# A transformer block with attention and eight experts on one core: sums of x from DRAM, a fourth pair buffer, one stay of tails, the fifth tile amid the chain

## The chip, the core and the metric

The kernel runs on one core of one Trainium2 chip. The core has five engines, each with its own instruction queue: TensorE (PE, matrix products into the eight PSUM banks), VectorE (DVE), ScalarE (ACT), GpSimd (POOL) and SyncE (SP, which here issues nearly all DMA). They meet through semaphores. The metric is the device time of one execution in microseconds (us), lower is better. The kernel before was timed three times: 2646.43 us in the median, 2645.69 to 2650.43 us.

## The reference

```python
xn = layernorm(x)                       # x: 1 x 2048 x 448, float32
# A: attention, 16 heads of 28
q, k, v = split(xn @ wqkv)              # wqkv: 448 x 1344
p = softmax(q @ k.T * 28 ** -0.5)       # 2048 x 2048 for each head
A = concat_heads(p @ v) @ wo            # wo: 448 x 448
# B: eight experts, all eight chosen (top 8 of 8)
gates = softmax(xn @ w_gate)            # 448 x 8
for e in range(8):
    B += gates[:, e] * (silu(xn @ w1[e]) @ w2[e])   # w1: 8 x 448 x 1792, w2: 8 x 1792 x 448
out = x + A + B
```

## The kernel before

**Numbers.** TensorE works in float16. To keep float32 quality each operand is split into a high and a low float16 part, and a product is the sum of three matmuls (high by high, high by low, low by high).

**Two streams.** After a first phase (norm of x, transposes, q, k, v, gates: about 110 us) two streams run side by side to the end. The *experts* go through 24 groups (`GROUPS`: three per expert, of 5, 5 and 4 tiles of 128 rows of w1) and in each group through 4 blocks of 512 tokens: 96 *units*. *Attention* goes through 256 tiles (one head, 128 queries), each in two halves of 1024 keys.

**A unit** (`unit`) computes four of the group's tiles for 512 tokens with a scheme of the Strassen kind on part of the inner dimension: seven products instead of eight, on sums of quarters of w1 (buffers `wa`) and sums of quarters of x (`T1` to `T4`, kept for all tokens in the tile `xt`). In the code's words: A11 into bank b1; ACT copies b1 to bank b2 (L1146); S1 into b3; ACT copies b3 to `s5` (L1148); S2 onto b1; DVE puts b1 + s5 into b3 (L1151); A12 onto b2; S3 onto b1; DVE puts b1 + s5 into b4 (L1155); S4 onto b3; A22 onto b1. This is called the *chain* here: each step on b1 has to wait until the copy or the sum before it has read b1. The products are L1105. The rest of the inner dimension goes on top as plain products (`plain`, L1121) and as *tails* (`tails`, L1132): the last 64 rows, which need only half of the PE's 128 rows, so that two such matmuls run in the two halves of the array at once. There are two stays of tails in a unit: b2 and b3 after S4, b1 and b4 at the end.

**After it** every bank goes through `silu`: ACT's tanh from the bank into a float32 tile `t` (L1202), DVE's (tanh + 1) times z (L1205, which frees the bank), ACT's high part `hh` (L1208), POOL's low part `hl` (L1209). A group of five has one more tile (`single`, L1177: 11 matmuls of 512 columns), which runs ahead of its unit. When a unit's parts stand, `summed` multiplies them by w2 for four token tiles (L1265, three matmuls of 448 columns for each tile of the group) and DVE adds the result, weighted by the gate, to `acc` (L1276).

**Weights.** While a group is computed, the next one's w1 and w2 are loaded, their largest magnitudes taken by DVE (L405) and brought to all partitions over DRAM (`mxs`, `scmg`), and then scaled and split by ACT and POOL (`split_w1`, `split_w2`). There are three `wa` buffers for pairs of tiles (`RWA`), two pairs in a group.

**Attention.** `score` writes 128 x 1024 scores into the two banks of kind "s" (L1363, two matmuls); DVE multiplies them by minus the scale in place and takes the minimum (L1367, a custom instruction with an accumulator that is then read out); ACT takes the exponential (L1383) and the high part (L1391); DVE the low part (L1386); SP transposes both by DMA (L1404); `weigh` multiplies by V (L1438 on four column strips of 32, L1445), `project` by wo (L1531).

**Order.** All instructions are jobs in a planner (`Plan`): a job has an engine, a cost in ns, a priority `v` (the units' and the attention's priorities are spread over the run), dependencies and buffers. At the kernel's build it plays the jobs through with these costs, gives each engine that falls free the ready job of lowest priority whose buffers fit, and writes the instructions in that order. On the chip every engine then works through its list as it stands. PSUM banks are given out by kind: "u" (b1, b3) any of 3, 2, 7, 6; "e" (b2, b4) 4 and 5; "z" and "y" 6, 7, 3, 2 (and more for "y").

## Time and profile before

| what | value |
|---|---|
| median of three runs | 2646.43 us (2645.69 to 2650.43) |
| the profiled execution's own time | 2647.7 us |
| its span, first to last instruction | 2645.9 us |
| granted TensorE clock | 0.999 |
| busy: PE, DVE, ACT, POOL | 2596.9, 2350.1, 2069.8, 1356.0 us |
| DMA: mean rate, share of the 16 engines in the main queue | 160 GB/s, 73.9% |

The rows that follow in the prediction come from that one execution. "L1105" is line 1105 of the kernel before. A row of groups reads: line, engine, operation, what it writes and reads, shape, count, busy time, mean ns of one, and the idle time of the engine ahead of it with what ended it. A row of the timeline reads: start, duration, engine, line, operation, shape, count, and in brackets an idle time. Matmuls follow each other before the one ahead has ended: the distance of two starts is what one costs, the duration is longer.

### The profile page before, as it was taken

Reading aid. Unit: us, or ns where it says so; the run is one execution under the profiler, and the core shown is the slowest. Engines: PE = TensorE matmul, PEld = TensorE weight load, DVE = VectorE, ACT = ScalarE, POOL = GpSimd, SP = SyncE. Lnnn points to the kernel's source line nnn. Section 1 sums busy time; section 2 is a strip of 40 time slices with the busy share of each in tenths; the row PEclk is TensorE's granted clock in tenths of the full one; section 3 lists DMA queues with packets and bytes.
Section 4 is the critical chain, followed back from the end, with each engine's and each line's share of the span. In section 5 each row is a group of like instructions: output and inputs, shape, how many; then the busy total and the mean of one; then the engine's idle time right before and its main releaser. Section 6 shows DMA issues by size and latency. Waiting matters only on the chain.

```text
span 2645.9 us, 54809 instructions
## 1 busy us (share of the span) xinstructions
PE 2596.9 (98%) x20863; PEld 1597.2 (60%) x20863; DVE 2350.1 (89%) x3567; ACT 2069.8 (78%) x2993; POOL 1356.0 (51%) x1377
## 2 busy tenths in 40 slices
PE   9999999999999999999999999999999999999999
PEld 4565665566656666556666656655566666656656
DVE  8779899998998899989999899998899998998873
ACT  5578778777887877888888877878778888787772
POOL 2345535544655444555454655555546555466462
PEclk9999999999999999999999999999999999999999
DMA  9657677687777778678887787877787677877741
GB/s 258 176 117 169 151 169 169 146 168 160 157 176 157 161 160 166 160 161 157 170 172 155 157 166 170 171 152 168 145 175 174 159 178 159 174 173 146 151 104 60
DMA packets 1237303, 424.46 MB, mean 160 GB/s; under 512 B 1156144, under 2 KB 1201712, under 8 KB 1237040
## 3 DMA queue, kind: packets, MB, share of 16 engines
q1 hardware_dynamic: 1236480, 420.94, 73.9%
q8 instruction: 164, 2.69, 0.5%
q14 instruction: 99, 0.81, 0.1%
q10 hardware_dynamic: 560, 0.02, 0.0%
HBM read 119.72 MB, written 15.23 MB: 51 GB/s over the span
## 4 chain that ended last, share of the span: by engine, by line
PE 54%; DVE 9%; ACT 3%; issue 2%; POOL 1%; DMA 1%; SPq 0%; DVEq 0%; POOLq 0%; ACTq 0%
PE banks L1265 22%; PE banks L1105 10%; PE banks L1121 8%; PE banks L1363 5%; PE banks L1177 3%; DVE banks L1367 3%; PE banks L1445 3%; DVE pl L1386 2%; PE banks L1438 2%; PE banks L1132 1%; DVE t L1205 1%; ACT pf L1383 1%; PE banks L1531 1%; DVE acc L1276 1%; ACT ph L1391 1%
## 5 line engine op out<-in xcount | busy, mean ns | idle before, releaser
L1209 POOL TENSOR_TENSOR hl<-t,hh 128x512 f16<-128x512 f32 x448 | 594.8, 1336 | 810.5 <-ACT hh L1208 753.6
L1265 PE MATMUL banks<-w,hh 128*128 128x448 f16 x3576 | 969.7, 353 | 2.2 <-DVE acc L1276 1.6
L1383 ACT ACTIVATE pf<-banks,mx 128x1024 f32<-128x1024 f32 x512 | 568.4, 1110 | 287.3 <-DVE mx L1367 248.7
L1386 DVE SCALAR_TENSOR_TENSOR pl<-pf,ph 128x1024 f16<-128x1024 f32 x512 | 719.4, 1407 | 39.7 <-ACT ph L1391 38.7
L1367 DVE CUSTOM_DVE_ANT_0 banks<-banks,zero,cneg 128x1024 f32<-128x1024 f32 x512 | 658.1, 1285 | 69.5 <-PE banks L1363 56.2
L1265 PE MATMUL banks<-w,hl 128*128 128x448 f16 x1788 | 630.2, 352 | 0.0
L1391 ACT ACTIVATE ph<-pf 128x1024 f16<-128x1024 f32 x512 | 539.0, 1053 | 4.9
L1265 PEld LDWEIGHTS <-hh 128*128 128x128 f16 x3576 | 339.9, 98 | 335.9 <-issue 27.4
L1105 PEld LDWEIGHTS <-wa 128*128 128x128 f16 x4032 | 391.9, 98 | 141.6 <-issue 42.4
L1121 PE MATMUL banks<-xs,wc 128*128 128x256 f16 x3072 | 399.0, 273 | 0.0
L1202 ACT ACTIVATE t<-banks,the 128x512 f32<-128x512 f32 x448 | 298.4, 681 | 101.3 <-POOL hl L1209 50.1
L1105 PE MATMUL banks<-xt,wa 128*128 128x256 f16 x2304 | 313.2, 273 | 26.7 <-ACT banks L1146 14.3
L1205 DVE SCALAR_TENSOR_TENSOR t<-t,banks 128x512 f32<-128x512 f32 x448 | 298.4, 680 | 46.1 <-ACT t L1202 45.1
L1121 PEld LDWEIGHTS <-wc 128*128 128x128 f16 x3072 | 294.3, 98 | 62.4 <-issue 15.8
L1363 PE MATMUL banks<-K,Q 112*128 112x512 f16 x1024 | 305.9, 380 | 11.2 <-ACT pf L1383 10.4
L1276 DVE SCALAR_TENSOR_TENSOR acc<-banks,gwe,acc 128x448 f32<-128x448 f32 x383 | 257.2, 677 | 59.0 <-PE banks L1265 58.1
L1208 ACT ACTIVATE hh<-t 128x512 f16<-128x512 f32 x448 | 273.9, 623 | 18.0 <-DVE t L1205 10.2
L1265 PEld LDWEIGHTS <-hl 128*128 128x128 f16 x1788 | 174.4, 98 | 164.2 <-POOL hl L1209 0.5
L1105 PE MATMUL banks<-xs,wa 128*128 128x256 f16 x1728 | 236.5, 273 | 0.0
L611 POOL TENSOR_TENSOR w<-r,w 128x448 f16<-128x448 f32 x112 | 136.5, 1228 | 76.2 <-ACT w L608 74.7
L1177 PE MATMUL banks<-xs,wc 128*128 128x512 f16 x704 | 164.9, 379 | 0.0
L1363 PEld LDWEIGHTS <-Q 112*128 112x128 f16 x1024 | 94.1, 98 | 83.7 <-issue 30.5
(173 smaller groups left out, 2603.7 us busy)
## 6 DMA issues: line engine op xcount, KB each, us to landing
K<-qk SPq DMA_DIRECT2D x512, 56.0 KB
r<-in_B_w_dram SPq DMA_DIRECT2D x16, 1120.0 KB
V<-vs SPq DMA_DIRECT2D x64, 256.0 KB
r<-in_B_w_dram SPq DMA_DIRECT2D x16, 960.0 KB
Q<-qk SPq DMA_DIRECT2D x256, 28.0 KB
r<-in_B_w_dram SPq DMA_DIRECT2D x8, 896.0 KB
r<-in_B_w_dram SPq DMA_DIRECT2D x8, 768.0 KB
r<-in_B_w_dram SPq DMA_DIRECT2D x32, 160.0 KB
```

The source lines that it names most:

```text
L1105: nc.tensor.matmul(bank()[:, q * HC : (q + 1) * HC], w, xx, start=(start and q == 0 and i == 0), stop=True, skip_group_check=True,)
L1121: nc.tensor.matmul(bank()[:, q * HC : (q + 1) * HC], ww, xx, start=False, stop=True, skip_group_check=True,)
L1202: add("ACT", 686, lambda: nc.scalar.activation(t(), z(), AF.Tanh, scale=th_()[:, 0:1]), v, r=[z, th_], w=[t])
L1205: lambda: nc.vector.scalar_tensor_tensor(t(), t(), 1.0, z(), op0=ALU.add, op1=ALU.mult),
L1209: add("POOL", 1159, lambda: nc.gpsimd.tensor_tensor(hl(), t(), hh(), ALU.subtract), v, r=[t, hh], w=[hl])
L1265: nc.tensor.matmul(y()[:, 0:D], a, wv, start=(i == 0 and u == 0), stop=(i == g - 1 and u == 2))
L1276: lambda: nc.vector.scalar_tensor_tensor(acc[:, n, :], y()[:, 0:D], gb()[:, n : n + 1], acc[:, n, :], op0=ALU.mult, op1=ALU.add),
L1363: nc.tensor.matmul(b()[:, cs], q()[:, q0 : q0 + P], k()[:, cs], start=True, stop=True)
L1367: nc.vector.tensor_tensor_reduce(b(), b(), zero.to_broadcast([P, 2 * C]), cneg, HUGE, op0=ALU.add, op1=ALU.min, accum_out=m()[:, n, j : j ...
L1383: nc.scalar.activation(p(), s(), AF.Exp, bias=m()[:, n, j : j + 1], scale=-1.0)
L1386: nc.vector.scalar_tensor_tensor(l()[:, js], p(), P_SCALE, h()[:, js], op0=ALU.mult, op1=ALU.subtract)
L1391: add("ACT", 1060, lambda: nc.scalar.activation(h()[:, js], p(), AF.Copy, scale=P_SCALE), v, r=[p], w=[(h, j)])
```

## The change

- **Sums of x.** `xt`, 16 KB in every partition, goes. The sums are worked out after the first phase (`sums_of_x`, now in `moe`), written to DRAM (`xd`), and each unit has its own 4 KB buffer out of two, loaded from `xd` (`sums_x`, 512 KB per load, 94 loads); the first two units get theirs directly.
- **Buffers.** `wa` 3 to 4, `w2` 6 to 7, `hh` and `hl` 7 to 8 (now rings in one tile `hr`), `t` 2 to 3.
- **Tails.** One stay at the end of a unit for all four banks, eight matmuls; all four `silu` follow it.
- **Fifth tile.** `single` stands between S1 and S2 of its unit.
- **Scores.** The scale is put into q and k when they are split. DVE takes the minimum of the raw scores by a `tensor_reduce` that writes nothing back.
- **Scales of weights.** w1 and w2 get theirs apart, w1's earlier; the splitting starts earlier; POOL's first part of a pair is three jobs. Some costs and constants of the planner differ.

```diff
-RWA, RWC, RW2, RH, RHC, RT, RPP, RPF = 3, 4, 6, 7, 2, 2, 2, 2
+RWA, RWC, RW2, RH, RHC, RT, RPP, RPF = 4, 4, 7, 8, 2, 3, 2, 2
...
-    mxs = dp.tile([len(GROUPS), P, 2], F32, name="mxs")
+    mxs = dp.tile([len(GROUPS), 2, P, 2], F32, name="mxs")
     vs = dp.tile([H, P, NC, TPC * 64], F16, name="vs")
+    xd = dp.tile([NC, P, 8, HC], F16, name="xd")
...
-    xt = mp.tile([P, 8 * XT], F16, name="xt")
+    hr = mp.tile([P, 2 * RH * C], F16, name="hr")
...
-                add("ACT", 600, lambda pq=pq, qh=qh: nc.scalar.activation(qh(), pq(), AF.Copy), v(), r=[pq], w=[qh])
+                def high(pq=pq, qh=qh, sc_=sc_):
+                    nc.scalar.activation(qh(), pq(), AF.Copy, scale=sc_)
+                def low(pq=pq, qh=qh, ql=ql, sc_=sc_):
+                    nc.vector.scalar_tensor_tensor(ql(), pq(), sc_, qh(), op0=ALU.mult, op1=ALU.subtract)
...
             v = go([b3], strassen(b3, S1, T1, True))
-            add("ACT", 610, lambda: nc.scalar.activation(s5(), b3(), AF.Copy), v, r=[b3], w=[s5])
+            add("ACT", 595, lambda: nc.scalar.activation(s5(), b3(), AF.Copy), v, r=[b3], w=[s5])
+            done = amid(last, v0) or done
             tick()
...
             go([b3], strassen(b3, S4, B22), plain(b3, 0, 1))
-            v = go([b2, b3], tails((b2, b3), 0))
-            silu(gi, b, (0, 0), b2, v)
-            silu(gi, b, (0, 1), b3, v)
             tick()
             go([b4], plain(b4, 1, 1))
             go([b1], strassen(b1, A22, T4), plain(b1, 1, 0))
-            v = go([b1, b4], tails((b1, b4), 1))
+            v = go([b2, b3, b1, b4], tails(((b2, 0, 0), (b3, 0, 1), (b1, 1, 0), (b4, 1, 1))))
+            silu(gi, b, (0, 0), b2, v)
+            silu(gi, b, (0, 1), b3, v)
             silu(gi, b, (1, 0), b1, v)
             silu(gi, b, (1, 1), b4, v)
...
+        def sums_x(gi, b, v):
+            XS_[gi, b] = x = buf("mp", [P, 8, HC], F16, f"xt{gi}_{b}", tag="xt", bufs=2)
+            if not gi and b < 2:
+                sums_of_x(b, x, v)
+                return
+            dma(lambda: x(), lambda: xd[b], v, r=[("xd", b, 0), ("xd", b, 1)], w=[(x, 0), (x, 1)], kb=512)
...
+                todo = [(SLOT_A, scale_w1, gi + 1)]
+                todo += [(SLOT_A + 2 + 2 * i, split_w1, gi + 1, i) for i in range(len(W1S[g1]))]
+                todo += [(SLOT_B, scale_w2, gi + 1)]
...
             for b in range(NC):
-                if g > 4:
-                    single(gi, b)
-                unit(gi, b, tick)
+                g1, b1 = (gi, b + 1) if b + 1 < NC else (gi + 1, 0)
+                if 0 < g1 < len(GROUPS) or b1 > 1:
+                    sums_x(g1, b1, at(spent[0]))
+                unit(gi, b, tick, lambda after, v: single(gi, b, after, v) if g > 4 else None)
...
-                nc.vector.tensor_tensor_reduce(
-                    b(), b(), zero.to_broadcast([P, 2 * C]), cneg, HUGE,
-                    op0=ALU.add, op1=ALU.min, accum_out=m()[:, n, j : j + 1],
-                )
-            add("DVE", 1292, top, v, r=["cexp"], w=[b, (m, n, j)], more=58)
+                nc.vector.tensor_reduce(m()[:, n, j : j + 1], b(), op=ALU.min, axis=AX.X)
+            add("DVE", 1215, top, v, r=[b], w=[(m, n, j)])
...
+V0 = 20.0
+AHEAD, SLOT_A, SLOT_B = 0.0, 1, 6
```

What this does to the order is shown at three places: the second unit of the run on PE, where the chain and the tails stand; a later unit's `silu` on ACT; and SP's queue. Lines of the kernel after the change have other numbers: there L1084 are the products of the chain, L1100 the plain ones, L1111 the tails, L1156 the fifth tile, L1408 the scores, L1446 the transposes of the exponentials.

On PE, the second unit before: the last product of A11 (it reads `xs`) and the first of S1 (S1 and S2, twelve products that read `xt`, follow each other with nothing between), and the first of its two stays of tails (`wc` are the plain weights of a pair of tiles).

```order
L1105 MATMUL banks<-xs,wa_2_978 128x256
L1105 LDWEIGHTS wa_0_954
L1105 MATMUL banks<-xt,wa_0_954 128x256
...
L1121 MATMUL banks<-xs,wc_2_1044 128x256
L1132 LDWEIGHTS wc_0_1005
L1132 MATMUL banks<-xs,wc_0_1005 128x256
...
L1132 MATMUL banks<-xs,wc_2_1044 128x256
L1121 LDWEIGHTS wc_0_1005
L1121 MATMUL banks<-xs,wc_0_1005 128x256
```

Between A11 and S2 there stand S1's six matmuls only. After the change the same unit, from the last product of S1 to the first of S2:

```order
L1084 MATMUL banks<-xt_1_861,wa_2_964 128x256
L1156 LDWEIGHTS wc_4_933
L1156 MATMUL banks<-xs,wc_4_933 128x512
...
L1408 MATMUL banks<-K_1_1500,Q_1468 128x512
L1156 LDWEIGHTS wc_4_933
...
L1156 MATMUL banks<-xs,wc_4_933 128x512
L1084 LDWEIGHTS wa_0_943
L1084 MATMUL banks<-xt_1_861,wa_0_943 128x256
```

The eleven matmuls of the fifth tile and a pair of scores now stand between S1 and S2; the unit's tails are one run of eight matmuls at its end.

On ACT, the second unit of the tenth group before, from the first tanh of its four banks to the last (`t_1_00` to `t_1_11`; `pf`, `ph` are exponentials, `hh` high parts):

```order
L1202 ACTIVATE t_1_00_14086<-banks,the_13587 128x512
L1391 ACTIVATE ph_14032<-pf_1_14068 128x1024
L1202 ACTIVATE t_1_01_14105<-banks,the_13587 128x512
...
L1208 ACTIVATE hh_1_00_14127<-t_1_00_14086 128x512
L1383 ACTIVATE pf_0_14130<-banks,mx_14108 128x1024
L1391 ACTIVATE ph_14140<-pf_0_14130 128x1024
L1202 ACTIVATE t_1_10_14148<-banks,the_13587 128x512
L1208 ACTIVATE hh_1_01_14175<-t_1_01_14105 128x512
L1383 ACTIVATE pf_1_14179<-banks,mx_14108 128x1024
L1208 ACTIVATE hh_1_10_14217<-t_1_10_14148 128x512
L1202 ACTIVATE t_1_11_14235<-banks,the_13587 128x512
```

and after (`r` and `wa` are the next group's weights, `hr` holds the high parts):

```order
L1240 ACTIVATE t_1_00_13928<-banks,the_12546 128x512
L1240 ACTIVATE t_1_01_13941<-banks,the_12546 128x512
L1240 ACTIVATE t_1_10_13943<-banks,the_12546 128x512
L553 ACTIVATE r_10_13371<-r_10_13371,scoa_13832 128x4x256
L580 ACTIVATE wa_2_13948<-r_10_13371 128x128
L580 ACTIVATE wa_2_13948<-r_10_13371 128x256
L1425 ACTIVATE pf_0_13972<-banks,mx_13501 128x1024
L1247 ACTIVATE hr<-t_1_00_13928 128x512
L1433 ACTIVATE ph_13985<-pf_0_13972 128x1024
L1247 ACTIVATE hr<-t_1_01_13941 128x512
L1240 ACTIVATE t_1_11_14008<-banks,the_12546 128x512
```

Three of the four tanh follow each other at once, the fourth comes seven instructions later; before they came one or two at a time.

On SP after the change, around one load of sums (`xt_0`, for the first unit of a group):

```order
L1446 DMA_TRANSPOSE tl_9745<-pl_9984 128x16x128
L1446 DMA_TRANSPOSE th_10194<-ph_10058 128x16x128
L382 DMA xt_0_10216<-xd 128x2048
L1446 DMA_TRANSPOSE tl_10294<-pl_10119 128x16x128
L1497 DMA_TRANSPOSE tt_10310<-lt_10297 128x4x128
L382 DMA V_10328<-vs 128x1024
```

Before, the transposes of two exponentials followed each other there, and no load of sums stood in the queue; now one stands ahead of a transpose in each unit.

## The prediction

> **What bounds the kernel now.** I read the page first, then PE's waits, then the timeline of one unit.

> ```profile
> span 2645.9 us, 54809 instructions
> PE 2596.9 (98%) x20863; PEld 1597.2 (60%) x20863; DVE 2350.1 (89%) x3567; ACT 2069.8 (78%) x2993; POOL 1356.0 (51%) x1377
> PE 54%; DVE 9%; ACT 3%; issue 2%; POOL 1%; DMA 1%; SPq 0%; DVEq 0%; POOLq 0%; ACTq 0%
> ```

> PE is busy for all but 49 us of the span, and it is 54% of the chain that ended last. DVE at 89% looks close to a bound, but the rows of its waits say that it waits for PE:

> ```profile
> DVE acc L1276 <- PE banks L1265: 58.1, 61, 2.2
> DVE banks L1367 <- PE banks L1363: 56.2, 72, 3.2
> ```

> So time is won only where PE stops or spends more than its columns need. Its own waits (us in total, times, longest), complete but for 3 us in small rows:

> ```profile
> PE banks L1105 <- ACT banks L1146: 14.3, 20, 1.9
> PE banks L1363 <- ACT pf L1383: 10.4, 11, 1.8
> PE banks L1105 <- DVE banks L1151: 9.9, 11, 1.8
> PE banks L1438 <- DVE u L1463: 2.8, 3, 1.9
> PE banks L1265 <- DVE acc L1276: 1.6, 2, 1.3
> PE banks L728 <- DVE one L722: 1.2, 1, 1.2
> PE banks L1105 <- DVE t L1205: 1.1, 1, 1.1
> ```

> Rows one and three, 24.2 us, are the chain: S2 waits until ACT has copied b1, S3 until DVE has read it. What a matmul costs, and what PE loses without a wait, stands in the timeline of a unit of the first group (start, duration, ...), its last row ACT's:

> ```profile
> 133.27 0.82 PE L1105 MATMUL banks<-xs,wa 128*128 128x256 f16 x6
> 133.92 0.82 PE L1105 MATMUL banks<-xt,wa 128*128 128x256 f16 x6
> 135.61 0.81 PE L1105 MATMUL banks<-xt,wa 128*128 128x256 f16 x6 [0.87 <-ACT banks L1146]
> 136.26 0.82 PE L1105 MATMUL banks<-xs,wa 128*128 128x256 f16 x6
> 141.93 1.04 PE L1121 MATMUL banks<-xs,wc 128*128 128x256 f16 x8
> 142.90 0.39 PE L1132 MATMUL banks<-xs,wc 64*128 64x256 f16 x4
> 143.23 0.55 PE L1265 MATMUL banks<-w,hh 128*128 128x448 f16 x2
> 134.98 0.58 ACT L1146 ACTIVATE banks<-banks 128x512 f32<-128x512 f32 x1
> ```

> Six matmuls of 256 columns take 0.65 (133.27 to 133.92), 0.109 each. S1 begins at 133.92 and S2 could follow at 134.57; it begins at 135.61. PE lost 1.04 there, where the bracket says 0.87: a stop costs some 0.16 more than its row, because the last matmul's modelled end covers that much. ACT began its copy at 134.98 and was through at 135.56: from the start of S1, 133.92, PE would have needed 1.7 us of other work. And the tails: eight plain matmuls from 141.93 are through at 142.80 (8 x 0.109), the tails begin at 142.90, 0.10 late; they need 2 x 0.109 = 0.22 (two at a time, in two halves of the array) and the next begins 0.33 later, 0.11 late. A stay costs 0.20 beside its work.

> **The change part by part.**

> *One stay of tails.* The matmuls are the same in number and width, and in the run of eight the halves still alternate, so pairs still run together. From 192 stays, 96 go: 96 x 0.20 = 19.2 us of PE time, on the engine that bounds. From below: if a stay of eight lost its pairing it would cost 4 x 0.109 more, which the unchanged order of halves excludes. I take -19.2.

> *Fifth tile amid the chain.* In the order before, 46 of the 96 units have less than 1.6 us of matmuls between the end of A11 and S2 (counted over the whole PE order, each matmul at its distance in the trace); after, 18 have. Between S2 and S3 24 units have less than that before, 9 after. S2's wait costs 14.3 + 20 x 0.16 = 17.5, S3's 9.9 + 11 x 0.16 = 11.7. Shrinking both in proportion saves 17.5 x 28/46 = 10.7 and 11.7 x 15/24 = 7.3: -18.0 us. The bounds are 0 (ACT and DVE are late for reasons of their own, whatever stands between) and -29.2 (all of it). I take the proportion: the wait quoted above stands where only S1 covers ACT's copy, and there the fifth tile's 11 matmuls and a score now stand.

> *The minimum of the scores.*

> ```profile
> L1367 DVE CUSTOM_DVE_ANT_0 banks<-banks,zero,cneg 128x1024 f32<-128x1024 f32 x512 | 658.1, 1285 | 69.5 <-PE banks L1363 56.2 <-ACT ph L1391 9.0 <-ACT s L1148 1.2
> L1367 DVE DVE_READ_ACCUMULATOR2_ANT mx<- 128x1 f32 x512 | 71.9, 140 | 0.0
> L405 DVE TENSOR_REDUCE mx<-r 128x1 f32<-128x1024 f32 x16 | 19.3, 1210 | 0.0
> 1002.30 1.29 DVE L1367 CUSTOM_DVE_ANT_0 banks<-banks,zero,cneg 128x1024 f32<-128x1024 f32 x1
> 1003.50 0.14 DVE L1367 DVE_READ_ACCUMULATOR2_ANT mx<- 128x1 f32 x1
> 1003.50 1.27 DVE L1276 SCALAR_TENSOR_TENSOR acc<-banks,gwe,acc 128x448 f32<-128x448 f32 x2
> 67.42 1.08 DVE L405 TENSOR_REDUCE mx<-r 128x1 f32<-128x896 f32 x1
> 68.41 0.41 DVE L858 TENSOR_SCALAR xa<-acc,rstd,shift 128x256 f32<-128x256 f32 x1
> ```

> By busy time 1285 + 140 becomes 1210: 215 ns x 512 = 110 us. But the next instruction starts 1.20 after the old one (1002.30 to 1003.50, the readout runs beside it), and 0.99 after a reduce of 896, so about 1.12 after one of 1024: DVE really wins 0.08 x 512 = 41 us, and the exponential starts 0.13 earlier (1.20 + 0.14 against 1.21). [...] On PE's time I count 0: DVE does not set the end, and the order puts scores closer (54 of 511 distances below 3.0 us of PE work, 35 before), which spends the shorter loop. Bounds: 0 and -(10.4 + 11 x 0.16) = -12.2, all waits of scores for the bank.

> *All four `silu` at the end of the unit.* ACT now has four tanh in a burst, and the four banks come free later against the next unit. Between the last tails and the next A11 there are less than 8 us of matmuls in 16 of 95 places (same count), before in 7; less than 10 us in 45, before in 20. The last tanh in the order shown stands behind these (mean ns after the busy time):

> ```profile
> L546 ACT ACTIVATE r<-r,scog 128x1024 f32<-128x1024 f32 (+1 forms) x64 | 66.3, 1035 | 15.4 <-DVE scog L440 15.2
> L573 ACT ACTIVATE wa<-r 128x128 f16<-128x128 f32 x96 | 29.6, 355 | 1.5
> L1383 ACT ACTIVATE pf<-banks,mx 128x1024 f32<-128x1024 f32 x512 | 568.4, 1110 | 287.3 <-DVE mx L1367 248.7
> L1391 ACT ACTIVATE ph<-pf 128x1024 f16<-128x1024 f32 x512 | 539.0, 1053 | 4.9
> L1202 ACT ACTIVATE t<-banks,the 128x512 f32<-128x512 f32 x448 | 298.4, 681 | 101.3 <-POOL hl L1209 50.1
> L1205 DVE SCALAR_TENSOR_TENSOR t<-t,banks 128x512 f32<-128x512 f32 x448 | 298.4, 680 | 46.1 <-ACT t L1202 45.1
> L1208 ACT ACTIVATE hh<-t 128x512 f16<-128x512 f32 x448 | 273.9, 623 | 18.0 <-DVE t L1205 10.2
> ```

> 4 x 0.68 + 1.04 + 2 x 0.36 + 1.11 + 1.05 + 2 x 0.62 = 7.9, and DVE's 0.68: 8.6 us until the last bank is free. Nine units more than before fall under that; the waiting instruction is A11 or S1 of the next unit, and the whole PE queue stands behind it. At the mean stop of the chain (14.3/20 + 0.16 = 0.88) nine cost 7.9. b1 and b3 may take any of four banks, and the third `t` takes away what ACT waits for POOL's `hl` (50.1 us in the row of L1202), so I take half: +4.0. Bounds: 0, and +16 (nine at the longest wait of PE, 1.8).

> *Sums of x from DRAM.*

> ```profile
> q1 hardware_dynamic: 1236480, 420.94, 73.9%
> L1146 ACT ACTIVATE banks<-banks x96: 577/582/603, 122.4 to 2616.6; 128x512 f32<-128x512 f32 x96
> 801.65 6.07 DMA scmg<-mxs
> 1032.12 0.58 SPq L381 DMA_DIRECT2D V<-vs x1
> PE banks L1438 <- DMA tl<-pl: 0.2, 1, 0.2
> ```

> 94 loads of 512 KB are 49 MB more in that queue; at its mean cost (73.9% for 420.94 MB) 8.7% more, 83%. A unit is (2616.6 - 122.4)/95 = 26.3 us long. The buffer falls free when the unit before last is through and is wanted one unit later, and the longest DMA piece that I found in the chain took 6.07: 20 us of cover. On SP a load takes about V's 0.58, and what stands behind it are transposes for which PE waited 0.2 us in the whole run. I take 0. Bounds: 0, and 94 x 0.58 = 54 if every one delayed PE by its issue.

> *The rest.* The scale in q and k is on 28 tiles in the first phase, where PE's own products of 512 columns cover ACT and DVE. The sums of x stood ahead of the units before as well. More buffers and earlier weights take away waits of ACT and POOL, not of PE. The last steps of the attention keep their distance (19.1 us of PE work between the last L1438 and wo, 19.3 before). I take 0.

> Sum on the span: 2645.9 - 19.2 - 18.0 + 4.0 = 2612.7. The median of the runs lies 0.5 above the profiled span (2646.4; that execution's own 2647.7 is 1.8 above). **Forecast: 2613 us.**

> **The rivals.**

> *Tails only.* The stops of the chain stay, at other places: ACT and DVE are late because their queues are, and PE's order, written from the planner's costs, meets them anyway. For it: in the quoted stop ACT began its copy 0.9 late, at 134.98, being at other work when A11 was through. Against it: 1.7 us would have covered even that, and the covers below 1.6 go from 46 to 18. 2646.4 - 19.2 = 2627.

> *Nearly all waits go.* Chain (29.2) and scores (12.2) both, by the shorter loop and the third `t`: 2646.4 - 19.2 - 29.2 - 12.2 = 2586. For it: DVE's 41 us; against it: scores stand closer.

> *Four banks at once: slower.* The next unit's A11 and S1 wait for `silu` in most units, as freeing the banks takes 8.6 us and the order leaves less than 10 in 45 of 95. It decides from 37.2/95 = 0.39 us per unit on, the sum of the two gains; at 0.53 (45 stops of 1.1, the one that the row has) it costs 50: 2646.4 - 37.2 + 50 = 2659. The row L1105 <- DVE t, one wait of 1.1 us, speaks against it. [...]

> *The loads come late.* The sums don't arrive a unit ahead, because SP's queue works in order and stands; S1 waits. At 0.58 in each of 94 units: 2646.4 - 37.2 + 54 = 2663.

> **How the numbers follow.** Forecast 0.68 (its own range 2601 to 2625), tails only 0.14, nearly all 0.08, banks 0.06, loads 0.04. The range runs to 2594 below, two thirds of the way to the faster rival, and to 2634 above, where the tails' gain alone meets half of the bank waits' bound: it leaves out most of the last three, some 0.17 in all. A measurement of this kernel can tell 0.2%, 5.3 us, from no change. The first three cases are all faster by more: 0.90. The last two decide around zero and beyond: 0.05 within 0.2%, 0.05 slower.

> **What would show it.** The tails' line has 96 stays of eight, and a stay of 0.44 + 0.20 instead of 2 x 0.42. PE's waits for ACT's copy of b1 fall to about 6 us, for DVE's b3 to about 4. DVE's busy time falls by about 110 us with the count of instructions down by 512 readouts. A row "PE <- DVE t" of more than 10 us means the third rival, a row "PE <- DMA xt" the fourth. If PE's waits in sum are still above 45 us, the second part of my sum is wrong.

## The result, and the profile after

The change is **slower**: 2674.56 us in the median of four runs (2672.75 to 2686.73) against 2646.76 for the kernel before (2645.69 to 2650.43), a ratio of 1.0115, 95% interval 1.0099 to 1.013. The forecast was 2613, so 62 us are missing. The page of the change (the profiled execution took 2686.7, 12 above the median, so its rows show somewhat more than the median loses): span, busy times, the main DMA queue (packets, MB, share of 16 engines), and the chain that ended last by engine.

```profile
span 2684.9 us, 54523 instructions
...
PE 2595.9 (97%) x20863; PEld 1620.9 (60%) x20863; DVE 2338.6 (87%) x3127; ACT 2065.9 (77%) x2993; POOL 1367.2 (51%) x1377
...
q1 hardware_dynamic: 1265248, 475.50, 89.0%
...
PE 49%; DVE 15%; DMA 8%; ACT 7%; issue 4%; POOL 1%; SPq 1%; DVEq 0%; ACTq 0%; POOLq 0%
```

PE is busy as long as before (2596.9), though 96 stays of tails are gone, and for 89.0 us it is not busy (49.0 before). DMA has 8% of the chain, 1% before; the queue stands at 89.0%, where the prediction had 83. PE's waits of the change (us in total, times, longest):

```profile
PE banks L1480 <- DMA tl<-pl: 31.6, 18, 5.6
PE banks L1487 <- DMA th<-ph: 10.9, 7, 2.6
PE banks L1408 <- ACT pf L1425: 6.8, 16, 1.2
PE banks L1084 <- ACT banks L1125: 4.3, 8, 0.9
PE banks L1084 <- DVE banks L1131: 4.1, 5, 2.2
```

The last two rows are the chain, 8.4 us where 24.2 stood: as forecast. New are the first two: 42.5 us of waits for SP's transposes of the exponentials, for which PE waited 0.2 us before. Around 780 us, SP's queue in the timeline of the change (start, duration), and then PE:

```profile
768.30 1.89 SPq L1446 DMA_TRANSPOSE th<-ph  x1
...
771.79 0.37 SPq L382 DMA_DIRECT2D xt<-xd  x1
772.25 6.80 SPq L1446 DMA_TRANSPOSE tl<-pl  x1
779.13 0.53 SPq L382 DMA_DIRECT2D scma<-mxs  x1
```

```profile
776.16 0.82 PE L1084 MATMUL banks<-xt,wa 128*128 128x256 f16 x6
...
782.55 1.90 PE L1480 MATMUL banks<-tl,V 128*32 128x512 f16 x16 [5.57 <-DMA tl<-pl]
784.38 1.03 PE L1408 MATMUL banks<-K,Q 112*128 112x512 f16 x2
...
789.80 0.60 PE L1408 MATMUL banks<-K,Q 112*128 112x512 f16 x2
```

A transpose stands in the queue for 6.80 us behind a load of the sums, and PE stops for 5.57. Two scores then take 1.03, where the two at 789.80 take 0.60. The same place by stretches (PE busy and count, ..., then the granted clock, DMA share, GB/s):

```profile
770.00:780.00 10.00, 6.98 (x98) 4.78 (x96) 8.39 (x10) 8.07 (x13) 6.54 (x6) 1.00 0.66 142
780.00:790.00 10.00, 7.45 (x53) 4.64 (x54) 3.78 (x8) 4.23 (x5) 2.19 (x1) 0.66 1.06 216
790.00:800.00 10.00, 10.00 (x67) 5.89 (x66) 9.68 (x15) 9.26 (x13) 7.87 (x11) 1.00 1.13 219
```

By the trace's record of the granted clock it is at half from 780.17 to 787.00, 6.8 us, of which the first 2.4 still lie in the stop. There are ten such stretches in the change, 47.8 us in sum (one of 3.4 before). PE works in 40.5 us of them; at half the clock that makes, as an estimate, some 20 us lost: about the 19.2 by which its busy time was to fall.

### The profile page after: what moved, and what is told of

Same layout as the page of the kernel before. It is cut to its first block, busy times and chain, and to the rows that moved or that the text cites. A ratio compares the mean times of both kernels' runs of the same rounds, so it can differ in the third digit from the quotient of the medians.

```text
span 2684.9 us, 54523 instructions
## 1 busy us (share of the span) xinstructions
PE 2595.9 (97%) x20863; PEld 1620.9 (60%) x20863; DVE 2338.6 (87%) x3127; ACT 2065.9 (77%) x2993; POOL 1367.2 (51%) x1377
## 4 chain that ended last, share of the span: by engine, by line
PE 49%; DVE 15%; DMA 8%; ACT 7%; issue 4%; POOL 1%; SPq 1%; DVEq 0%; ACTq 0%; POOLq 0%
PE banks L1305 19%; PE banks L1084 9%; PE banks L1100 8%; PE banks L1408 5%; DMA tl<-pl 5%; DVE pl L1428 4%; DVE mx L1412 4%; PE banks L1156 3%; DVE t L1243 2%; PE banks L1487 2%; PE banks L1480 2%; ACT pf L1425 2%; DVE acc L1316 2%; ACT ph L1433 2%; ACT t L1240 1%
## 5 line engine op out<-in xcount | busy, mean ns | idle before, releaser
L1305 PE MATMUL banks<-w,hr 128*128 128x448 f16 x5364 | 1083.8, 353 | 0.8 <-DVE t L1243 0.4
L1249 POOL TENSOR_TENSOR hr<-t,hr 128x512 f16<-128x512 f32 x448 | 602.1, 1358 | 603.1 <-ACT hr L1247 594.9
L1305 PEld LDWEIGHTS <-hr 128*128 128x128 f16 x5364 | 517.8, 98 | 495.1 <-issue 24.3
L1412 DVE TENSOR_REDUCE mx<-banks 128x1 f32<-128x1024 f32 x512 | 622.0, 1215 | 76.5 <-PE banks L1408 61.1
L1084 PEld LDWEIGHTS <-wa 128*128 128x128 f16 x4032 | 394.1, 98 | 121.1 <-issue 16.7
L1100 PE MATMUL banks<-xs,wc 128*128 128x256 f16 x3072 | 399.1, 274 | 3.6 <-DVE banks L1135 3.2
L1100 PEld LDWEIGHTS <-wc 128*128 128x128 f16 x3072 | 301.5, 98 | 67.5 <-issue 9.6
L1240 ACT ACTIVATE t<-banks,the 128x512 f32<-128x512 f32 x448 | 288.3, 684 | 60.8 <-PE banks L1111 47.3
L1084 PE MATMUL banks<-xt,wa 128*128 128x256 f16 x2304 | 316.0, 273 | 8.6 <-ACT banks L1125 4.3
L1408 PE MATMUL banks<-K,Q 112*128 112x512 f16 x1024 | 308.4, 382 | 11.4 <-ACT pf L1425 6.8
L1316 DVE SCALAR_TENSOR_TENSOR acc<-banks,gwe,acc 128x448 f32<-128x448 f32 x383 | 255.4, 674 | 46.1 <-PE banks L1305 45.7
L1247 ACT ACTIVATE hr<-t 128x512 f16<-128x512 f32 x448 | 270.8, 630 | 21.5 <-DVE t L1243 21.0
L1084 PE MATMUL banks<-xs,wa 128*128 128x256 f16 x1728 | 237.8, 274 | 0.2 <-ACT lt L1495 0.2
L561 POOL TENSOR_TENSOR wc<-r,wc 128x512 f16<-128x512 f32 x64 | 86.3, 1348 | 210.2 <-ACT wc L557 203.1
L1156 PE MATMUL banks<-xs,wc 128*128 128x512 f16 x704 | 166.4, 382 | 3.7 <-DVE acc L1316 2.1
L1408 PEld LDWEIGHTS <-Q 112*128 112x128 f16 x1024 | 94.7, 98 | 86.7 <-issue 30.1
L1487 PEld LDWEIGHTS <-th 128*128 128x128 f16 x4096 | 120.6, 97 | 30.8 <-DMA th<-ph 11.7
```

What stands on the lines that cost most here:

```text
L1084: nc.tensor.matmul(bank()[:, q * HC : (q + 1) * HC], w, xx, start=(start and q == 0 and i == 0), stop=True, skip_group_check=True,)
L1100: nc.tensor.matmul(bank()[:, q * HC : (q + 1) * HC], ww, xx, start=False, stop=True, skip_group_check=True,)
L1240: add("ACT", 686, lambda: nc.scalar.activation(t(), z(), AF.Tanh, scale=th_()[:, 0:1]), v, r=[z, (th_, 0)], w=[t])
L1249: add("POOL", 1159, lambda: nc.gpsimd.tensor_tensor(hl(), t(), hh(), ALU.subtract), v, r=[t, hh], w=[hl])
L1305: nc.tensor.matmul(y()[:, 0:D], a, wv, start=(i == 0 and u == 0), stop=(i == g - 1 and u == 2))
L1316: lambda: nc.vector.scalar_tensor_tensor(acc[:, n, :], y()[:, 0:D], gb()[:, n : n + 1], acc[:, n, :], op0=ALU.mult, op1=ALU.add),
```

## The experiments

Four theories are named in the expectations, each written before its run. TRAFFIC: the 94 loads make SP's queue late. ORDER (later PLAN): the planner's new order brings the waits, whatever the parts are worth. BUFFERS: what counts is the number of buffers. ALIGN, formed after the first four runs: where the transposes' tiles begin in memory sets what a packet costs. "Fifth tile" is `single`; "aligned" means that `ph` and `pl`, the sources of SP's transposes, begin at a multiple of 256 bytes.

**The loads, the buffers, the due times.** Sums kept in memory, without loads, and with the buffers of before:

```diff
-RWA, RWC, RW2, RH, RHC, RT, RPP, RPF = 4, 4, 7, 8, 2, 3, 2, 2
+RWA, RWC, RW2, RH, RHC, RT, RPP, RPF = 3, 4, 6, 7, 2, 2, 2, 2
-            XS_[gi, b] = x = buf("mp", [P, 8, HC], F16, f"xt{gi}_{b}", tag="xt", bufs=2)
+            if gi:
+                XS_[gi, b] = XS_[0, b]
+                return
+            XS_[gi, b] = x = buf("mp", [P, 8, HC], F16, f"xt{gi}_{b}", tag=f"xt{b}")
...
-            dma(lambda: x(), lambda: xd[b], v, r=[("xd", b, 0), ("xd", b, 1)], w=[(x, 0), (x, 1)], kb=512)
```

(The buffer counts go back to make room for the resident sums; the size of `hr` goes with them.)

> The changed kernel with the sums of x kept in SBUF for all tokens: no write to DRAM and none of the 94 loads; the buffers go back to the counts of the kernel before (three pair buffers, six of w2, seven of hh and hl, two of t), as the memory asks. Tails, fifth tile, minimum and scales stay changed. Theory TRAFFIC (the loads share SP's queue and the 16 DMA engines with the transposes of the exponentials, which land late for PE's product with their low parts and, after long stops, leave PE at half clock): 2605 to 2625 us, main queue back at 73 to 75%, PE waits for DMA tl and th under 2 us. Theory ORDER (the new order itself, four banks at once, stops PE): 2655 us or more, with the queue at 74% all the same.

2675.81 us (ratio 1.0119, 1.0103 to 1.0134). Then the change with its loads and, of that diff, only the line of the buffers:

> The changed kernel with its loads, but with the buffer counts of the kernel before, as in the run with resident sums; the two differ in the loads alone. TRAFFIC: 2665 to 2695 us, main queue near 89%, PE waits for DMA tl and th of 30 us or more. ORDER or BUFFERS (the additional buffers make the difference): within 10 us of the run with resident sums.

2701.59 (1.0214, 1.0198 to 1.0229). The kernel before with 94 loads of 512 KB that nothing reads:

```diff
+                if gi or b > 1:
+                    add(
+                        "SP", 400, lambda b=b, e=e: nc.sync.dma_start(xl[b], w1[e, 0:P, 0:1024]), at(spent[0]),
...
+                    )
```

> The kernel before with 94 loads of 512 KB added that nobody reads: one for each unit, issued when the products before that unit stand, 128 rows of 4 KB from w1 into a scratch tensor in DRAM, on SP's queue. Nothing else is changed. TRAFFIC: 2670 to 2700 us, main queue at 85 to 90%, new PE waits for DMA tl and th of 25 us or more. ORDER: 2642 to 2652 us.

2690.69 (1.017, 1.0153 to 1.0187). And the change with a planner that takes the transposes to land later (`TURN` 4500 to 7000 ns):

> The changed kernel, where the planner is told that a transpose lands 7.0 us after its transfer instead of 4.5, so that the products with the transposed exponentials stand later in PE's order. The traffic is the same. If TRAFFIC acts by late landings that the order does not allow for: PE waits for DMA tl and th fall to under 15 us and the time to 2625 to 2650. If the queue as a whole does not keep up: 2665 us or more.

2663.14 (1.0074, 1.0048 to 1.01): the waits for `tl` fell to 3.0 us and those for `th` to 6.8, but at the end PE waited 9.9 for `ohl` (the transposed result of the attention) and the clock stood at half for the last 25.7 us.

Without any loads the change was as slow. That alone does not clear the loads, because this run has the small buffers as well; but its packets were as slow too, and the aligned change below keeps all 94 loads and takes 2618. The loads do cost something (26 us between the first two runs; 46 on the kernel before, in an order of its own, where scores' waits for exponentials grew from 10.4 to 26.0). What remained was a row that no theory had: packets of 256 bytes in the main queue (1.12 million; the 512 transposes of 512 KB make 1.05 million of them) took 20.6 ns in the mean before and 23.8 to 24.0 in the change and in all its variants, loads or not, against 21.3 in the kernel before with loads. The median is 18 ns in both; the 90th percentile went from 18 to 27, and the packets above 20 ns from 22,000 to 166,000. What the variants share is the place of the tiles, as the built programs have it:

```
                 ph begins at byte   above a multiple of 256
kernel before          170240                  0
the change             171456                192
```

`pl`, `th` and `tl` lie behind `ph` at whole multiples of 256, so all four share this offset, and in each variant of the change without the unused bytes of the next part it is the same 192. It comes from the sizes of all buffers ahead of them.

**Alignment.** 64 unused bytes in each partition in the change, 192 in the kernel before; neither moves an instruction in the order (here the line of the change; in the kernel before it reads `[P, 48]`):

```diff
-    sc_o = mp.tile([P, 1], F32, name="sc_o")
+    mp.tile([P, 16], F32, name="pad"); sc_o = mp.tile([P, 1], F32, name="sc_o")
```

> The changed kernel with one unused tile of 64 bytes per partition ahead of the attention's tiles, so that the tiles of the exponentials (source and target of the transposes by DMA) begin at a multiple of 256 bytes, as in the kernel before, and not 192 above one. The order of instructions is the same, instruction by instruction. Theory ALIGN (a transpose's packets of 256 bytes take longer where the tiles are not aligned to 256): packets of 256 bytes back from 24.0 to 21 ns, main queue at 82 to 85%, time 2630 to 2655 us, PE waits for DMA tl and th under 12 us. Theory TRAFFIC alone: 2668 to 2680 us and 24 ns, as without the tile.

> The kernel before with one unused tile of 192 bytes, so that the same tiles begin 192 above a multiple of 256. Same order of instructions. ALIGN: packets of 256 bytes at 23 to 24 ns, main queue at 80 to 82%, PE waits for DMA tl and th that were 0.2 us, time 2655 to 2685 us. TRAFFIC alone: 2640 to 2650 us, 20.6 ns.

The change with 64 bytes: **2617.98** (0.9895, 0.988 to 0.9909), faster than before, and by more than ALIGN had said. The kernel before with 192: 2668.2 (1.0087, 1.0066 to 1.0108), its packets at 23.5 ns. Its queue (73.9% without the bytes) and the wait that was 0.2:

```profile
q1 hardware_dynamic: 1236480, 420.94, 80.0%
```

```profile
PE banks L1438 <- DMA tl<-pl: 8.6, 7, 3.8
```

The page of the aligned change, and its waits:

```profile
span 2614.7 us, 54523 instructions
...
PE 2572.8 (98%) x20863; PEld 1613.6 (62%) x20863; DVE 2331.2 (89%) x3127; ACT 2062.9 (79%) x2993; POOL 1372.8 (53%) x1377
...
q1 hardware_dynamic: 1265248, 475.50, 84.4%
```

```profile
PE banks L1480 <- DMA tl<-pl: 8.4, 4, 3.8
PE banks L1408 <- ACT pf L1425: 4.3, 10, 0.7
PE banks L1084 <- ACT banks L1125: 3.3, 7, 0.8
PE banks L1084 <- DVE banks L1131: 2.3, 4, 0.7
```

The same bytes and packets, but the queue is busy for 0.844 x 2614.7 = 2207 us instead of 0.890 x 2684.9 = 2390, 183 less; 1.12 million packets on 16 engines at 2.5 ns less (24.0 to 21.5) make 176. PE's busy time falls by 23.1, most of it the half clock (PE works 3.4 us in it instead of 40.5), and its time without work from 89.0 to 41.9. The third run puts the version without loads at a multiple of 256:

> The run with resident sums (no loads, buffer counts as before) with the tiles aligned to 256 by 64 unused bytes. ALIGN: main queue at 73 to 75%, PE waits for DMA tl from 12.9 to under 3 us, time 2645 to 2662 us; the 30 us that PE loses between 100 and 200 us, where scores wait for the exponentials, stay. ORDER: 2670 us or more.

2661.06 (1.0055, 1.004 to 1.007). Its missing gain is a matter of buffers, below. Then source and target apart, by an unused tile between `pl` and `th` (64 bytes alone for the targets; 64 ahead and 192 between for the sources):

```diff
-                nc.vector.scalar_tensor_tensor(
+                (i, j) == (0, 0) and pools.get("ap").tile([P, 16], F32, name="pad2", tag="pad2"); nc.vector.scalar_tensor_tensor(
```

> The change with 64 unused bytes per partition between pl and th: the targets th and tl of SP's transposes begin at a multiple of 256 bytes, the sources ph and pl stay 192 bytes above one. The order of instructions is the change's. TARGET (writing a packet of 256 bytes across a border costs): mean packet of 256 bytes 21 to 22 ns, 2616 to 2630 us, as with all four shifted. SOURCE (reading across a border costs): 23.5 to 24.5 ns, 2660 to 2680. Both halves matter: 22.5 to 23, 2630 to 2650.

> The change with 64 unused bytes ahead of the attention's tiles and 192 between pl and th: the sources ph and pl of SP's transposes begin at a multiple of 256 bytes, the targets th and tl 192 bytes above one. The order of instructions is the change's. TARGET: mean packet of 256 bytes 23.5 to 24.5 ns, 2660 to 2680 us. SOURCE: 21 to 22 ns, 2616 to 2630. Both: 22.5 to 23, 2630 to 2650.

Targets alone aligned: 2669.05 (1.0076, 1.0058 to 1.0095). Sources alone: **2613.23** (0.9876, 0.9859 to 0.9892), the fastest kernel of this study. PE's waits for the transposes, first in the run with the targets aligned, then in that with the sources aligned:

```profile
PE banks L1480 <- DMA tl<-pl: 29.1, 21, 4.9
...
PE banks L1487 <- DMA th<-ph: 7.8, 5, 3.7
```

```profile
PE banks L1480 <- DMA tl<-pl: 6.8, 5, 2.5
...
PE banks L1487 <- DMA th<-ph: 1.3, 1, 1.3
```

It is the reading side: packets at 24.1 ns with the targets aligned, 21.5 with the sources. (Every tile ahead of `th` moves with the sources, by the same 64 bytes; that the transposes' packets are the slow ones follows from their number, 93% of those of 256 bytes.) The mean rises from 21.5 to 24.1 ns in the change, 12%, and from 20.6 to 23.5 in the kernel before, 14%, and most packets stay at 18 ns. Sources began at 0 or at 192 bytes above a multiple of 256 in these runs and nowhere else, so from which offset on it costs is not shown, nor what a slow packet spends the time on.

**Parts alone.** With alignment known, are the prediction's terms there? On the kernel before, sources aligned throughout, first one stay of tails alone:

```diff
-            v = go([b2, b3], tails((b2, b3), 0))
-            silu(gi, b, (0, 0), b2, v)
-            silu(gi, b, (0, 1), b3, v)
...
-            v = go([b1, b4], tails((b1, b4), 1))
+            v = go([b2, b3, b1, b4], tails(((b2, 0, 0), (b3, 0, 1), (b1, 1, 0), (b4, 1, 1))))
+            silu(gi, b, (0, 0), b2, v)
+            silu(gi, b, (0, 1), b3, v)
```

> The kernel before with one stay of tails, all four silu behind it; nothing else, tiles aligned. The prediction's first and third term alone: -19.2 for 96 stays and up to +16 for the banks, 2628 to 2642 us. If emptying four banks at once bounds: 2660 us or more, with PE waits for DVE t above 10 us.

2664.99 (1.0071, 1.0056 to 1.0086). The fifth tile amid the chain alone:

```diff
+            done = amid(last, v0) or done
             tick()
...
-                if g > 4:
-                    single(gi, b)
-                unit(gi, b, tick)
+                unit(gi, b, tick, lambda after, v: single(gi, b, after, v) if g > 4 else None)
```

> The kernel before with the fifth tile amid the chain and nothing else; two stays of tails; the tiles of the transposes begin at a multiple of 256 bytes as before. The prediction's second term alone: 2646 - 18 = 2628 us (2617 to 2646 by its bounds); PE's waits for ACT's copy of b1 about 6 (14.3 before), for DVE's b3 about 4 (9.9 before). ORDER (the waits move to other places, as in the run with one stay alone): 2640 to 2660, with other rows of PE <- ACT or DVE banks of the same sum.

2688.65 (1.0155, 1.0139 to 1.017). Both, with the plain minimum and the scale in q and k:

> The kernel before with three parts of the change: one stay of tails, the fifth tile amid the chain, the plain minimum of the scores with the scale in q and k; 32 unused bytes keep the four tiles of the transposes at a multiple of 256 bytes. No loads, the buffers as before (two of t, three of wa). ALIGN with the sum of the prediction (the sums carry over): 2608 to 2625 us, one stay of 0.64 in 96 units, S2's and S3's waits about 13 in sum. BUFFERS (with one stay the four silu need the third t and the fourth wa): 2640 to 2668, with rows PE <- DVE t and PE <- ACT banks above 15 in sum, as in the run with one stay alone (2665).

2642.48 (0.9983, 0.9974 to 0.9992), within the bound of 0.2%. PE's longest rows of waits, with one stay alone and then with the fifth tile alone:

```profile
PE banks L1362 <- ACT pf L1382: 21.0, 21, 3.6
PE banks L1121 <- DVE banks L1155: 11.4, 8, 3.1
PE banks L1105 <- ACT banks L1146: 7.4, 19, 0.9
PE banks L1105 <- DVE banks L1151: 4.8, 8, 1.2
PE banks L1105 <- DVE t L1204: 4.6, 3, 2.2
```

```profile
PE banks L1363 <- ACT pf L1383: 52.4, 22, 6.3
PE banks L1121 <- DVE banks L1156: 5.3, 4, 4.0
PE banks L1105 <- ACT banks L1146: 4.9, 8, 1.7
PE banks L1105 <- DVE banks L1152: 4.0, 5, 1.4
```

The chain's waits fall as forecast (14.3 to 4.9 and 9.9 to 4.0 with the fifth tile), but scores now wait 21 to 52 us for exponentials (10.4 before), and half clock comes on top (31 and 58 us). So the signs named ahead did not come: with one stay the row PE <- DVE t is 4.6, not above 10, though the time is that of the slow case; the fifth tile alone is slower than either of its ranges; and with all three parts the long row is again scores waiting for exponentials (25.4), while PE <- DVE t and PE <- ACT banks make 7 in place of 15.

**Buffers or plan.** The aligned change with the buffers of before, then with two `t` in place of three, nothing else (the first diff's line of buffers, and this one's); then the aligned change, and the kernel before, with the due times of the experts' work (`M_AT`) beginning at 58 us in place of 60:

```diff
-RWA, RWC, RW2, RH, RHC, RT, RPP, RPF = 4, 4, 7, 8, 2, 3, 2, 2
+RWA, RWC, RW2, RH, RHC, RT, RPP, RPF = 4, 4, 7, 8, 2, 2, 2, 2
...
-M_AT, A_AT, LEAD, END, LAND, TURN = 60.0, 0.0, 130.0, 2585.0, 3500, 4500
+M_AT, A_AT, LEAD, END, LAND, TURN = 58.0, 0.0, 130.0, 2585.0, 3500, 4500
```

> The change with loads, but the buffers as before (three pair buffers, two t, six of w2, seven of hh and hl), and 64 unused bytes so that the transposes' sources begin at a multiple of 256 bytes; the planner orders it anew. BUFFERS (the larger buffers take 40 us of waits of scores for exponentials away): 2645 to 2665 us, with PE <- ACT pf above 25. PLAN (any new order costs some 10 to 40): the same time, so this run alone doesn't tell; the shifted due times do. Buffers worth nothing, as the prediction had it: 2613 to 2622.

> The change with two t in place of three, all else as in the change, the sources of the transposes at a multiple of 256 bytes; ordered anew. BUFFERS: 2630 to 2650 if the third t is half of what the buffers give, 2618 to 2622 if the fourth pair buffer is what counts. PLAN: 2625 to 2660, and no nearer to the change than the run with shifted due times.

> The change, sources of the transposes at a multiple of 256 bytes, with the due times of the second part's work beginning at 58 us in place of 60 (they end where they ended): the same work, buffers and transfers in another order. PLAN (the constants fit one order): 2630 to 2665, with more waits of scores for exponentials (15 to 45 us against 4). BUFFERS (the order is as good wherever it falls): 2612 to 2624, that row below 10.

> The kernel before with the due times of the second part's work beginning at 58 us in place of 60, nothing else; the sources of the transposes where they were. PLAN: 2655 to 2690 us, the waits of scores for exponentials at 20 to 50 against 10.4. BUFFERS: 2640 to 2652.

Buffers as before: 2668.11 (1.0085, 1.0069 to 1.01), 50 us above the aligned change. Two `t`: 2641.11 (0.9981, 0.9972 to 0.999), 23 above. Other due times: 2628.71 (0.9946, 0.9927 to 0.9965), 11 above, and for the kernel before 2650.81 (1.0021, 1.0012 to 1.003), 5 above. So one new order of the same work cost 5 us in one kernel and 11 in the other. Neither theory has both signs: the change lies between the two ranges, with its scores waiting 8.0 us for exponentials, as BUFFERS had it; the kernel before lies in the range of BUFFERS, with 24.8 us of such waits, as PLAN had it. The buffers cost more than either order, 23 and 50. Where two `t` lose it, PE's timeline of that run shows:

```profile
132.21 0.60 PE L1408 MATMUL banks<-K,Q 112*128 112x512 f16 x2
132.64 1.04 PE L1100 MATMUL banks<-xs,wc 128*128 128x256 f16 x8
133.61 0.61 PE L1111 MATMUL banks<-xs,wc 64*128 64x256 f16 x8
135.27 0.59 PE L1408 MATMUL banks<-K,Q 112*128 112x512 f16 x2 [1.04 <-ACT pf L1425]
138.39 0.69 PE L1408 MATMUL banks<-K,Q 112*128 112x512 f16 x2 [2.53 <-ACT pf L1425]
141.62 1.01 PE L1408 MATMUL banks<-K,Q 112*128 112x512 f16 x2 [2.53 <-ACT pf L1425]
145.16 1.01 PE L1408 MATMUL banks<-K,Q 112*128 112x512 f16 x2 [2.53 <-ACT pf L1425]
148.70 1.01 PE L1408 MATMUL banks<-K,Q 112*128 112x512 f16 x2 [2.53 <-ACT pf L1425]
```

Where the two streams begin to run side by side, PE's list holds nothing but scores for 25 us, each waiting for the exponential ahead of it, and the clock stays at half for 37.5 us. Of that run's 25.2 us of such waits 22.3 lie between 100 and 200 us; the four runs of versions of the change with the buffers of before have 21.9 to 23.9 there, the versions with three `t` have 1.2 at most. The kernel before, with two `t`, has none either, so it is two `t` in the change's order that does it; why the planner finds nothing else ready there was not followed up.

**Terms taken out of the aligned change.** Two stays of tails as before; and the fifth tile ahead of the chain as before (the two diffs above, turned round, in the change with 64 unused bytes):

> The change with two stays of tails as before, all else as in the change, the sources of the transposes at a multiple of 256 bytes; ordered anew. TERMS (the sum's terms hold where the buffers are large): 2618 + 19.2 - 4 = 2633 us, PE's busy time up by some 15, no new wait above 5. PLAN (only this one order is good): 2625 to 2660, the difference in waits of scores for exponentials. The term is worth nothing: 2615 to 2622.

> The change with the fifth tile ahead of the chain as before, all else as in the change, the sources of the transposes at a multiple of 256 bytes; ordered anew. TERMS: 2618 + 18 = 2636 us, PE's waits for ACT's copy of b1 up from 3.3 to about 14 and for DVE's b3 from 2.3 to about 10. PLAN: 2625 to 2660 with those waits below 6 and the difference in waits of scores for exponentials. The term is worth nothing: 2615 to 2622.

Two stays: 2625.71 (0.9923, 0.9907 to 0.994), 7.7 above the aligned change. Fifth tile ahead: 2623.0 (0.9914, 0.9899 to 0.9929), 5.0 above. Each is no more than a new order cost with nothing taken out (11 us in this kernel), and both runs are ordered anew, so the two net gains are not shown to be the parts' own. The page of the run with two stays, and the waits of the run with the fifth tile ahead:

```profile
span 2620.3 us, 54564 instructions
...
PE 2591.7 (99%) x20863; PEld 1597.0 (61%) x20863; DVE 2346.4 (90%) x3127; ACT 2062.4 (79%) x2993; POOL 1369.3 (52%) x1377
```

```profile
PE banks L1408 <- ACT pf L1425: 10.7, 19, 2.5
...
PE banks L1084 <- ACT banks L1125: 4.3, 11, 0.8
...
PE banks L1084 <- DVE banks L1130: 1.3, 3, 0.8
```

## Why the prediction was wrong

**The step that failed: "Sums of x from DRAM ... I take 0".** It priced the added loads (queue at 83%, an issue of 0.58, 20 us of cover) and took the transposes behind them to be what they were, "for which PE waited 0.2 us in the whole run". In the change PE waits 42.5 us for them, and some 20 us are lost to half clock behind its stops. The load of the queue was about right: at aligned sources it stands at 84.4%, and loads against resident sums, with the same small buffers and both aligned, cost 2668.1 - 2661.1 = 7 us, no more than a new order may cost. (With the large buffers no run goes without loads, so their price there is open.) What had no term at all, there or in "The rest", is that the new set of buffers moves the transposes' sources to 192 bytes above a multiple of 256:

| kernel | aligned | 192 bytes above | difference |
|---|---|---|---|
| before | 2646.8 | 2668.2 | 21.4 |
| change, sums resident, buffers as before | 2661.1 | 2675.8 | 14.7 |
| change, buffers as before | 2668.1 | 2701.6 | 33.5 |
| the change | 2618.0 | 2674.6 | 56.6 |

The price is higher where the queue is fuller (84.2 and 84.4% aligned in the last two rows, 73.9 and 75.1 in the first two), and at equal load where PE waits less for other things; four pairs show this, no more. Aligned, the change takes 2618 or 2613, so the forecast of 2613 was nearly the time of a kernel that differs from this one in unused bytes alone. That doesn't make its sum right:

- **"I take -19.2" (one stay of tails).** The size is right as PE time: with two stays PE is busy for 2591.7, with one for 2572.8, 18.9 less. In the aligned change's trace a stay of eight takes 0.54 and begins 0.10 late, the 0.64 of the forecast. But PE's time without work rises from 28.6 to 41.9, 13.3 where "+4.0" stood. That is inside its bound of 16, yet not by its mechanism: waits for `silu`'s `t` rise by 1.7 only, those for transposes by 5.4, for the chain by 3.1, for `acc` by 3.0. Net about 6, by the medians 7.7, where 15.2 was forecast.
- **"-18.0 us" (fifth tile amid the chain).** Mis-sized: 5.0 at most, and not from the chain. The chain's waits are at 5.6 in the aligned change, below the forecast (6 and 4), but also with the fifth tile ahead (4.3 and 1.3): there something else in the change had already taken them away. What differs are scores that wait for exponentials, 10.7 against 4.3. On the kernel before, the tile's place does what was said to these two rows, and the scores take back more. Which of the other parts takes the chain's waits away in the change was not tried.
- **"More buffers ... take away waits of ACT and POOL, not of PE" (The rest, 0).** Wrong by the most in the other direction: all of them are worth 50 us in the aligned change, the third `t` alone 23, each read from one order. In none of the runs with the small buffers did the prediction's two gains come; that the sum came near the aligned change's time is luck, errors that cancel, and the parts don't add up singly.
- **The minimum of the scores, 0.** One reduce takes 1215 ns as taken (1210), but no run took it out alone, so the time stays open. The forecast that DVE's busy time falls by 110 is wrong: 2350.1 to 2338.6. Of the 110 the read-outs made 71.9 and ran beside the next instruction, as the prediction's own rows had it. Added up one by one, DVE's instructions in the change are 83 us shorter; its busy time counts overlapping ones once and so falls by 11.5. Over 128 x 1024 the reduce takes 1215 ns in the change's trace, the step that forms `pl` 1421.
- **The rivals.** "The loads come late" (2663) named the right queue and a near time, but not the mechanism: no wait of PE for `xt` stands in the profile, and with all its loads the aligned change takes 2618. "Four banks at once" has the time of one stay on the kernel before, 18 us slower, but its sign only in part: 4.6 us for `silu`, beside 11.4 for DVE's sum and 10.6 more for scores. In the aligned change `silu`'s rows make 4.3 us in all.
- **What would show it.** "If PE's waits in sum are still above 45 us, the second part of my sum is wrong": they are 84.2 (44.0 before), but the second part's rows fell as forecast and the excess lies elsewhere. The sign was too coarse to say which step failed; the rows were not.

## What to carry to other kernels

When a change alters any buffer's size, look where the sources of DMA transposes begin afterwards: in these kernels an offset of 192 bytes cost 15 to 57 us, more where the queue was fuller, and 64 unused bytes bought it back. Compare the mean time of one packet of equal size between two traces before explaining a fuller queue by traffic. And a part that loses alone may gain in company (and the reverse): the terms of a sum hold only with the buffers and the order beside which they were read.
